# Attention and two MoE layers on one core: the second token block worked in two halves, the value sums taken by a selector product, and a new order of the work

## The chip, the cores and the metric

The kernel runs on one core of one Trainium2 chip, and the metric is the device time of one execution in microseconds (us). The engines are TensorE (PE, with its weight loads PEld), VectorE (DVE), ScalarE (ACT), GpSimd (POOL) and SyncE (SP), whose queue issues every DMA of this kernel. Each engine takes its own instructions in the order in which they are recorded, and waits on semaphores for the others.

## The reference

Eight heads of 64, two batches of 768 positions. A query sees the 31 positions nearest to it and, for every block of 32 positions, one summary: the block's maximal key (with log 32 added to the score) and the block's mean value. Two MLPs follow on all 1536 tokens of 512 columns.

```python
def _attn_ref(q, k, v):
    k_sum = k.reshape(B, H, nb, block, D).max(axis=3)
    v_sum = v.reshape(B, H, nb, block, D).mean(axis=3)
    scores_l = where(|i - j| < 16, q @ k.T / 8, -1e9)
    scores_s = q @ k_sum.T / 8 + log(32)
    a = softmax([scores_l, scores_s])          # sum + 1e-9
    return a @ [v, v_sum]
def _moe_ref(x, w_in, w_out):                  # 512 -> 2048 -> 512
    h = maximum(x @ w_in, 0); return (h * h) @ w_out
def _moe2_ref(x, w_in, w_out, g_ln):           # 512 -> 1024 -> 512
    h = x @ w_in; s = h * softmax(h)
    return ((s - mean(s)) / sqrt(var(s) + 1e-6) * g_ln) @ w_out
```

## The kernel before

**Blocks and units.** The 1536 tokens are three blocks of 512. Block 0 lies in batch 0, block 1 is the last 256 tokens of batch 0 and the first 256 of batch 1, block 2 lies in batch 1. Attention goes by units: a block and one of four pairs of heads. A unit needs its queries, the keys of its batch (loaded once per batch and pair, `load_k`), windows of values (`load_v`, into one of three buffers `vw`), and 24 rows of value sums, which `place_vs` copies under the values by DMA.

**Value sums.** `load_vst` brings 96 partitions (24 blocks by 4 heads) of 1024 numbers, half the positions of each block, into a buffer `kl` that it shares with the keys (two buffers in turn). `prep_vs` reduces them on DVE (L260), adds the second half (L262) and scales (L263). A unit holds two heads, one from each group of four, so its sums need all four loads of the batch.

**A unit's chain.** Scores of both heads on PE into two PSUM tiles (S), masking and row minimum on DVE (R, L310), exponentials on ACT (E, L318), reciprocal of the sum and scaling (n, N), transposes on PE (T) and their copy (C), products with the values (V), and the split of the result into a rounded part on ACT (H) and a residue on DVE (X). All MoE products use three terms: rounded by rounded, rounded by residue, residue by rounded.

**Weights.** They are stored as 64-bit words; each tile of 128x512 passes through ACT (a, L401), four DVE operations (b, c, d, e: L404, L408, L415, L418), a rounding (F) and a residue (f).

**First MoE.** `passes` names (block, phase) pairs; phases hold 6, 6 and 4 of the 16 column groups of the hidden layer. A step is 12 products `mm1` (M, L468), relu (U), square and residue (G, D), and 12 products `mm2` (O, L497) of 512 columns into four accumulators; 48 steps in all.

**Second MoE.** Twelve tiles of 128 tokens. `ysplit` (z) rounds a tile on ACT and takes its residue on POOL; `mm3` is 24 products (L543); `solu` (u) is a chain on DVE and ACT with one power on POOL (L566); `ln_tr` is eight transposes (L580); `mm4` is 24 products (L603). From tile 1 on the loop in `moe2` writes the order; tile 0 (i0, i1) stands in the table.

**What sets the order.** The table `ORDER`, written out by hand or planner, is recorded token by token: a letter (above), a number, and for some the engine (`d` DVE, `a` ACT, `p` POOL). `lk`, `lq`, `lv`, `ls`, `l` are loads, `y` a value sum, `P` `place_vs`, `k`, `K`, `m`, `q`, `Q`, `w` the preparation of keys and queries. `B4` is four products of the identity with itself (`warm`, L298) that nobody reads. SP issues the loads in the same order, with waits for the buffer to be free.

Of the kernel before, what the change touches and what calls it, by code (L numbers as in the profile page):

```python
# [21 lines left out]
ls0 lk0 lq0 lg0 l0 y0d lv0 B4 k0 lk1 k1 K0d K1d lq1 B1 q0 m0 ls1 Q0d w0a B7 S0 R0 l1 a0 R1 E0 b0 c0 d0 lv1 E1 e0 n0  # L22
N0d F0a n1 B14 k2 N1d k3 T0 K2d f0p lk2 T1 K3d C0a q1 m1 C1a lq2 Q1a y1d w1p l2 a1 b1 B8 S1 ls2 c1 d1 lv2 e1 F1d R2
f1p B5 k4 R3 E2 k5 K4d lk3 B1 q2 K5d E3 m2 lq3 n2 l3 N2d a2 n3 w2a B6 T2 y2d N3p C2a Q2a b2 ls3 c2 B6 S2 d2 e2 R4 F2a
B1 k6 k7 K6a f2d lk4 K7a R5 B1 q3 E4 lq4 Q3d m3 a3 E5 n4 w3p l4 y3d N4p B13 k8 k9 P0 K8a n5 N5d K9a ls4 B1 q4 lk5 m4
Q4a b3 l5 a4 w4p B4 V0 P1 T3 y4d H0 lv3 T4 C3a C4a B1 S3 lq5 X0 c3 k10 R6 K10a ls5 a5 R7 B2 V1 P2 E6 d3 T5 e3 k11 C5a
n6 l6 N6d E7 lk6 b4 B3 T6 b5 lq6 c4 q5 d4 C6a F3a n7 N7d H1 B2 V2 e4 K11a P3 Q5a c5 S4 lv4 f3p m5 H2 a6 y5d T7 F4a w5p
C7a l7 R8 ls6 f4p lq7 B7 V3 R9 E8 d5 k12 k13 e5 K12a q6 lk7 K13a n8 X1 F5a N8p H3 X2 lv5 E9 f5p X3 B4 T8 m6 M0 a7 n9
w6p y6d C8a l8 Q6a lq8 S5 U0a N9d G0 ls7 k14 b7 M1 b6 K14a c6 D0p R10 lv6 R11 E10 c7 k15 d6 T9 E11 e6 q7 O0 F6d l9 d7
C9a n10 Q7a N10d lq9 U1a n11 e7 G1 M2 N11d f6d a8 D1p y7d F7a K15a f7p T10 l10 a9 S6 C10a m7 P4 U2a q8 G2 R12 w7p M3  # L30
lq10 R13 E12 D2p E13 V4 P5 U3d n12 T11 a10 w8p O1 lv7 H4 C11a X4 Q8a b9 N12p P6 V5 n13 G3 N13d b8 T12 c8 H5 T13 c9
C12a O2 d8 C13a e8 X5 F8a lv8 D3d f8d S7 P7 d9 e9 q9 w9a R14 O3 lq11 R15 l11 E14 F9d f9d P8 b10 V6 Q9a c10 E15 d10 M4
e10 lv9 n14 H6 n15 F10a N14p X6 a11 l12 N15d T14 f10p U4d S8 C14d G4 b11 M5 R16 w10p P9 R17 E16 D4d l13 q10 a12 c11
# [26 lines left out]
def attn_moe_kernel(ctx, tc, q, k, v, w_in, w_out, w2_in, w2_out, g_ln, out):  # L60
# [13 lines left out]
    GB = 4  # L74
    NFC = DFF // P
# [42 lines left out]
    ap = actx.enter_context(tc.tile_pool(name="ap", bufs=1, side="right"))  # L118
    rctx = ExitStack()
# [4 lines left out]
    def consts():  # L124
        make_identity(nc, ident)
        nc.gpsimd.memset(mhalf, -0.5)
        nc.gpsimd.memset(one, 1.0)

        nc.gpsimd.memset(strip[:, :, 0:WK], 0.0)
        nc.gpsimd.memset(strip[:, :, WK:WN], 8.0 * LOGB)  # L130
        for h in range(2):
            r = strip[64 * h:64 * h + 64, :, 0:WK]

            nc.gpsimd.affine_select(out=r, in_=r, compare_op=ALU.is_gt, fill=-8.0 * BIG, base=0,
                                    pattern=[[0, 3], [1, WK]], channel_multiplier=-1)
# [18 lines left out]
    units = [(t, hp) for t in range(NT) for hp in range(HP)]  # L154

    segs = []
    for t in range(NT):
        segs.append([])
        lo = t * TB
        while lo < (t + 1) * TB:  # L160
            hi = min((t + 1) * TB, (lo // S + 1) * S)
            segs[t].append((lo // S, lo % S, (lo - t * TB) // 64, (hi - lo) // 64))
            lo = hi

# [39 lines left out]
    def prep_q0(u):  # L204
# [40 lines left out]
    def prep_vs(i, pool=False):
        b, h, half = i // 4, i // 2 % 2, i % 2
        n = HP * NSUM
        x = vst_t.pop(i)[0:n]
        if i % 4 == 0:
            vs[b] = ap.tile([n, 2, D], F32, name="vs", bufs=2)  # L250
        s = vs[b][:, h]
        o = s if half == 0 else ap.tile([n, D], F32, name="vs1", bufs=2)
        if pool:
            w = 512
            while w >= D:
                r = o if w == D else x[:, 0:w]
                nc.gpsimd.tensor_tensor(out=r, in0=x[:, 0:w], in1=x[:, w:2 * w], op=ALU.add)
                w //= 2
# [42 lines left out]
    EDGE = {(0, 0): 1, (1, 0): 1, (1, GB - 1): 2, (2, GB - 1): 2}  # L301

    def att_r(g):
        t, hp = units[g // 2]
        ps = ps_t.pop(g)
# [408 lines left out]
```

## Time and profile before

| | us |
|---|---|
| three runs | 514.0, 514.32, 516.18 (median 514.32) |
| the profiled execution, device time | 514.84 |
| its span in the trace | 512.7 |
| PE busy | 485.4 (95%), 2990 products |
| DVE busy | 349.5 (68%) |
| ACT busy | 236.0 (46%) |
| POOL busy | 127.0 (25%) |

The first product of the first MoE (M0) starts at 68.57 us, and attention and MoE products are mixed until about 158 us. From 161 us to the end of the first MoE at 372 us, and from 390 us to 509.6 us, PE has hardly a gap. A share over the whole span therefore hides that the first 70 us are another stage: there PE is busy with fillers (`warm` is 182 of the records, 26.9 us), while DVE is busy 97% of the time from 20 to 40 us.

### The profile page before, as it was taken

What the parts mean: (1) busy time and instruction counts of PE and PEld (TensorE: products, weight loads), DVE (VectorE), ACT (ScalarE), POOL (GpSimd) and SP (SyncE); (2) the same over time, 40 slices, a digit from 0 to 9 for tenths busy, and PEclk for the clock granted to TensorE, in tenths of its full rate; (3) what the DMA queues carried; (4) which work ended last, traced back from release to release, by engine and by line L of the source; (5) the groups of instructions that cost most, each with busy time, mean ns of one, the idle gap of its engine ahead of it and who ended that gap; (6) DMA issues with size and microseconds to landing.
All of it is one profiled execution on the core that took longest, in us unless ns stands there. A gap on an engine that the chain in (4) does not pass through costs nothing.

```text
span 512.7 us, 8027 instructions
## 1 busy us (share of the span) xinstructions
PE 485.4 (95%) x2990; PEld 405.5 (79%) x2990; DVE 349.5 (68%) x748; ACT 236.0 (46%) x526; POOL 127.0 (25%) x137
## 2 busy tenths in 40 slices
PE   6787787999999999999999999999999999999997
PEld 5786666787878888888888888888777888888886
DVE  4996997698971569962017979979187877665560
ACT  2464786679682545243235544575422242222231
POOL 2223443331210225112224244332312211210000
PEclk9897999999999999999999999999999999999999
DMA  8988889474720043360000514322000001000011
GB/s 176 239 208 187 187 196 223 89 175 140 189 57 0 2 123 83 105 179 4 0 1 0 166 42 124 122 91 75 0 2 0 22 21 42 20 22 20 22 41 41
DMA packets 59590, 44.03 MB, mean 86 GB/s; under 512 B 46624, under 2 KB 49184, under 8 KB 59552
## 3 DMA queue, kind: packets, MB, share of 16 engines
q1 hardware_dynamic: 59552, 43.53, 33.9%
q8 instruction: 23, 0.38, 0.3%
q14 instruction: 15, 0.12, 0.1%
HBM read 39.19 MB, written 3.15 MB: 83 GB/s over the span
## 4 chain that ended last, share of the span: by engine, by line
PE 68%; DVE 8%; DMA 8%; issue 5%; SPq 5%; ACT 4%; POOL 1%; ACTq 0%; POOLq 0%
PE acc L497 21%; PE h L468 21%; PE po L603 13%; PE h L543 8%; DMA st<-in_moe_w_in_dram 4%; PE lt L580 2%; DMA vw<-vs 2%; SPq L201 2%; DVE vs L260 1%; DMA kl<-in_v_dram 1%; PE at L349 1%; DMA kl<-in_k_dram 1%; SPq L174 1%; ACT sm L318 1%; ACT wf L401 1%
## 5 line engine op out<-in xcount | busy, mean ns | idle before, releaser
L468 PE MATMUL h<-xh,wi 128*128 128x512 f32 x384 | 128.5, 396 | 1.6 <-ACT r L475 1.6
L497 PE MATMUL acc<-gh,wo 128*128 128x512 f32 x384 | 126.6, 391 | 0.0
L468 PEld LDWEIGHTS h<-xh,wi 128*128 128x128 f32 x384 | 72.8, 190 | 17.3 <-ACT r L475 1.8
L497 PEld LDWEIGHTS acc<-gh,wo 128*128 128x128 f32 x384 | 72.1, 188 | 15.1 <-issue 0.2
L468 PE MATMUL h<-xl,wi 128*128 128x512 f32 x192 | 75.2, 392 | 0.0
L497 PE MATMUL acc<-gl,wo 128*128 128x512 f32 x192 | 74.8, 389 | 0.0
L89 POOL TENSOR_TENSOR gl<-r,gh 128x512 fp32r<-128x512 f32 x29 | 39.5, 1361 | 138.7 <-ACT r L484 96.0
L543 PE MATMUL h<-w,wf 128*128 128x512 f32 x288 | 67.8, 390 | 1.4 <-POOL wf L89 0.6
L543 PEld LDWEIGHTS h<-w,wf 128*128 128x128 f32 x288 | 53.8, 188 | 13.5 <-POOL wf L89 1.1
L483 ACT ACTIVATE gh<-r 128x512 fp32r<-128x512 f32 x48 | 30.3, 631 | 54.8 <-DVE r L477 44.5
L401 ACT ACTIVATE wf<-st 128x512 f32<-128x512 f32 x48 | 31.9, 669 | 29.5 <-DMA st<-in_moe_w_in_dram 19.5
L477 DVE TENSOR_SCALAR r<-h 128x512 f32<-128x512 f32 x22 | 15.1, 687 | 41.7 <-PE h L468 41.7
L468 PEld LDWEIGHTS h<-xl,wi 128*128 128x128 f32 x192 | 36.5, 190 | 7.2
L497 PEld LDWEIGHTS acc<-gl,wo 128*128 128x128 f32 x192 | 36.1, 188 | 7.2
L418 DVE SCALAR_TENSOR_TENSOR wf<-st,wf 128x512 uint32<-128x512 uint32 x48 | 40.5, 850 | 1.1
L318 ACT ACTIVATE sm<-sm,mn 128x120 f32<-128x120 f32 x96 | 36.5, 386 | 7.9 <-DVE mn L310 7.9
L553 ACT ACTIVATE st<-h,nm 128x1024 f32<-128x1024 f32 x12 | 13.4, 1117 | 56.8 <-DVE nm L550 56.8
L415 DVE SCALAR_TENSOR_TENSOR wf<-st,wf 128x512 uint32<-128x512 uint32 x48 | 34.1, 713 | 0.9
L566 POOL TENSOR_TENSOR vr<-vr,mhalf 128x1 f32<-128x1 f32 x12 | 6.6, 550 | 111.2 <-DVE vr L565 111.2
L475 ACT ACTIVATE r<-h 128x512 f32<-128x512 f32 x26 | 15.5, 597 | 35.5 <-PE h L468 35.5
L484 ACT ACTIVATE r<-r 128x512 f32<-128x512 f32 x48 | 30.4, 633 | 1.5
L603 PE MATMUL po<-wo,lh 128*128 128x512 f32 (+1 forms) x104 | 30.1, 373 | 0.0
(112 smaller groups left out, 787.4 us busy)
## 6 DMA issues: line engine op xcount, KB each, us to landing
st<-in_moe_w_out_dram SPq DMA_DIRECT2D x24, 512.0 KB, 4.2
st<-in_moe_w_in_dram SPq DMA_DIRECT2D x32, 256.0 KB, 4.0
st<-in_moe_w_in_dram SPq DMA_DIRECT2D x8, 512.0 KB, 3.7
kl<-in_v_dram SPq DMA_DIRECT2D x8, 384.0 KB, 5.0
kl<-in_k_dram SPq DMA_DIRECT2D x16, 192.0 KB, 4.5
out_dram<-ob SPq DMA_DIRECT2D x11, 256.0 KB, 2.0
vw<-in_v_dram SPq DMA_DIRECT2D x16, 168.0 KB, 2.9
qr<-in_q_dram SPq DMA_DIRECT2D x16, 128.0 KB, 5.4
```

The source lines that it names most:

```text
L89: eng.tensor_tensor(out=lo, in0=x, in1=hi.bitcast(F32), op=ALU.subtract)
L318: nc.scalar.activation(out=sm[:, j], in_=sm[:, j], func=AF.Exp, bias=mn[:, j:j + 1], scale=-1.0, accum_out=su[:, j:j + 1])
L401: nc.scalar.activation(out=wf_t[n], in_=st_t[n].rearrange("p (n t) -> p n t", t=2)[:, :, 1], func=AF.Abs)
L415: nc.vector.scalar_tensor_tensor(out=w, in0=st[:, :, 0], scalar=29, in1=w, op0=ALU.logical_shift_right, op1=ALU.bitwise_or)
L418: nc.vector.scalar_tensor_tensor(out=w, in0=st[:, :, 1], scalar=0xC0000000, in1=w, op0=ALU.bitwise_and, op1=ALU.bitwise_or)
L468: nc.tensor.matmul(ps, wi[:, wsel, d, :], x[t][:, d, :], start=(n == 0), stop=(n == 3 * HP - 1))
L475: nc.scalar.activation(out=r_t[s], in_=h_t.pop(s), func=AF.Relu)
L483: nc.scalar.activation(out=gh, in_=r, func=AF.Square)
L484: nc.scalar.activation(out=r, in_=r, func=AF.Square)
L497: nc.tensor.matmul(acc_t[e], wo[:, wsel, e, :], x, start=(edge(s, -1) and i == 0), stop=(edge(s, 1) and i == 2))
L543: nc.tensor.matmul(h2[:, fs], x[:, c, :], w_t[NW1 + nh * NDC + c][:, wsel, :], start=(n == 0), stop=(n == 3 * NDC - 1))
L603: nc.tensor.matmul(po[:, ds], x[:, cs], w_t[NW1 + 8 + c][:, wsel, ds], start=(n == 0), stop=(n == 3 * NF2 - 1))
```

## The change

- `TOK` gives attention four blocks: 512, 256, 256 and 512 tokens. The two of 256 are the old block 1, cut at the border of the batches; their units have one group of four score blocks (both heads) instead of two. There are 16 units and, as before, 24 groups. `passes` runs the first phase of block 1 in two halves of 256 columns (6 steps each), so the steps are 54; later phases of block 1 are whole.
- The value sums: one load per batch and pair of heads, 96 partitions of 2 x 512 numbers; three halving additions on DVE or POOL (`sum_v0`); a product of a 96x24 selector with entries 1/32 (`sum_v1`); a copy of 24x128 numbers (`sum_v2`). A unit's sums need its own load alone. Of the eight chains of additions three are on DVE and five on POOL.
- The transposes of the first block's probabilities go to an accumulator tile instead of one of the three tiles `at`.
- `ysplit` is cut in two tokens, so that the residue of a tile (`Z`) has a place of its own in the table.
- `ORDER` is new from the first token to the second MoE; fillers go from 91 products to 24.

```diff
-ls0 lk0 lq0 lg0 l0 y0d lv0 B4 k0 lk1 k1 K0d K1d lq1 B1 q0 m0 ls1 Q0d w0a B7 S0 R0 l1 a0 R1 E0 b0 c0 d0 lv1 E1 e0 n0
+ls0 lk0 l0 lq0 y0d B3 j0 lk1 J0d k0 k1 K0d K1a m0 a0 b0 c0 B5 q0 l1 d0 e0 lq1 w0a Q0a B2 S0 lk2 k2 k3 R0 E0 K2d ls1
...
-f45p O45 U46d b47 G46 f46p c47 M47 D46d d47 e47 g47 z0 i0 F47a U47a f47p G47 O46 D47d z1 i1 O47 z2 u0 Ya47 Yd47
+g46 i1 G53 D53d a47 b47 f45p F46d f46d z1 z2 c47 d47 e47 Z2p u0 O53 Yd53 g47 Z1p F47a f47p Ya53
...
+    TOK = (0, TB, S, 2 * TB, 3 * TB)
...
+        nc.gpsimd.memset(sel, 1.0 / 32.0)
...
+        nc.sync.dma_start(out=x[0:HP * NSUM].rearrange("p (h x) -> p h x", h=2),
+                          in_=ap_of(v[b, hp], 0, [[8 * D, HP * NSUM], [HP * S * D, 2], [1, 8 * D]]))
+
+    def sum_v0(i, eng):
+        x = vst_t[i][0:HP * NSUM].rearrange("p (h r d) -> p h r d", h=2, d=D)
+        for r in (4, 2, 1):
+            eng.tensor_tensor(out=x[:, :, 0:r], in0=x[:, :, 0:r], in1=x[:, :, r:2 * r], op=ALU.add)
+
+    def sum_v1(i):
+        b, hp = i // HP, i % HP
+        x = vst_t.pop(i)[0:HP * NSUM].rearrange("p (h r d) -> p h r d", h=2, d=D)
+        ps = acc_tile() if i < HP else ps_at.tile([P, 512], F32, name="at")
+        kq_t["v", i] = ps
+        nc.tensor.matmul(ps[32 * hp:32 * hp + NSUM, 0:P], sel, x[:, :, 0], start=True, stop=True)
+
+    def sum_v2(i, eng):
...
+        eng(vs[b][r], kq_t.pop(("v", i))[r, 0:P])
...
-        else:
-            nc.vector.tensor_reduce(out=o, in_=x.rearrange("p (j d) -> p d j", d=D), op=ALU.add, axis=AX.X)
-        if half == 1:
-            nc.vector.tensor_tensor(out=s, in0=s, in1=o, op=ALU.add)
-            nc.vector.tensor_scalar(out=s, in0=s, scalar1=1.0 / 32.0, scalar2=None, op0=ALU.mult)
...
-        ps = ps_at.tile([P, 512], F32, name="at")
+        ps = acc_tile() if units[groups[g][0]][0] == 0 else ps_at.tile([P, 512], F32, name="at")
...
-    passes = [(0, 0), (1, 0), (2, 0), (2, 1), (1, 1), (0, 1), (0, 2), (1, 2), (2, 2)]
-    steps = [(pi, sum(PHASE[:ph]) + i) for pi, (t, ph) in enumerate(passes) for i in range(PHASE[ph])]
+    HALF = ((1, 0, TB // 2), (1, TB // 2, TB))
+    FULL = tuple((t, 0, TB) for t in range(NT))
+    passes = [(x, 0) for x in FULL[:1] + HALF + FULL[2:]] + [(FULL[t], ph) for ph, t in ((1, 2), (1, 1), (1, 0), (2, 0), (2, 1), (2, 2))]
+    steps = [(x, sum(PHASE[:ph]) + i) for x, ph in passes for i in range(PHASE[ph])]
...
-                nc.tensor.matmul(ps, wi[:, wsel, d, :], x[t][:, d, :], start=(n == 0), stop=(n == 3 * HP - 1))
+                nc.tensor.matmul(ps[:, 0:hi - lo], wi[:, wsel, d, :], x[t][:, d, lo:hi], start=(n == 0), stop=(n == 3 * HP - 1))
...
-        split_lo(nc.gpsimd, yl, src, yh)
+        yhl[i] = (yh, yl, src)
+
+    def ysplit_lo(i, eng):
+        yh, yl, src = yhl[i]
+        split_lo(eng, yl, src, yh)
         yhl[i] = (yh, yl)
```

Three places show how the order moves. The first is DVE at the start, from the first value sum to the first masking of scores (ISA), as it was; kl is the loaded values, kT and ks keys and their block maxima, qT queries, wf a weight tile.

```order
L260 TENSOR_REDUCE vs<-kl 96x64
L631 COPY kT_93<-acc_167 128x384
L631 COPY kT_93<-acc_174 128x384
L191 TENSOR_REDUCE ks_98<-kT_93 128x24
L631 COPY qT_103<-acc_184 128x512
L310 ISA sm,mn<-at,strip 128x120
```

And as it is after the change:

```order
L242 TENSOR_TENSOR kl<-kl 96x2x256
L242 TENSOR_TENSOR kl<-kl 96x2x128
L242 TENSOR_TENSOR kl<-kl 96x2x64
L676 COPY vs<-acc_167 24x128
L676 COPY kT_94<-acc_174 128x384
L207 TENSOR_REDUCE ks_99<-kT_94 128x24
L440 TENSOR_SCALAR wf<-wf 128x512
L444 TENSOR_SCALAR wf<-wf 128x512
L451 SCALAR_TENSOR_TENSOR wf<-st,wf 128x512
L454 SCALAR_TENSOR_TENSOR wf<-st,wf 128x512
L337 ISA sm,mn<-at,strip 128x120
```

The reduction is three additions, one copy of keys and the copy of queries have gone to ACT, and the first weight tile stands ahead of the scores instead of behind them.

The second is POOL where the second MoE begins, before. A wf on the left with y on the right is the residue of a tile of 128 tokens (tiles 0, 1, 2, 3 in the order of the rows, y being the first block's output); vr is the power in the chain of `solu` of tile 0, then of tile 1; wo is the residue of a weight tile.

```order
L89 TENSOR_TENSOR wf_3676<-y_1774,wf_3675 128x512
L89 TENSOR_TENSOR wo_3695<-wf_3632,wo_3695 128x512
L89 TENSOR_TENSOR wf_3718<-y_1774,wf_3717 128x512
L89 TENSOR_TENSOR wf_3746<-y_1774,wf_3745 128x512
L566 TENSOR_TENSOR vr_3763<-vr_3763,mhalf_60 128x1
L89 TENSOR_TENSOR wf_3811<-y_1774,wf_3810 128x512
L566 TENSOR_TENSOR vr_3828<-vr_3828,mhalf_60 128x1
```

After the change, where tile 0 is wf_3818, tile 1 is wf_3916 and tile 2 is wf_3919:

```order
L94 TENSOR_TENSOR wf_3818<-y_1707,wf_3817 128x512
L94 TENSOR_TENSOR wo_3888<-wf_3769,wo_3888 128x512
L94 TENSOR_TENSOR wf_3919<-y_1707,wf_3918 128x512
L610 TENSOR_TENSOR vr_3939<-vr_3939,mhalf_60 128x1
L94 TENSOR_TENSOR wf_3916<-y_1707,wf_3915 128x512
L94 TENSOR_TENSOR wo_3961<-wf_3908,wo_3961 128x512
L94 TENSOR_TENSOR wf_4004<-y_1707,wf_4003 128x512
L610 TENSOR_TENSOR vr_4021<-vr_4021,mhalf_60 128x1
```

The residue of tile 1 has moved from two places ahead of the power of tile 0 to the place right behind it; that of tile 2 is ahead of it still.

The third is PE at the first products of tile 1 (the loop's first), after the change; PE's rows are the same in both kernels there, apart from numbers. acc are the last accumulations of the first MoE, h2 the hidden layer of the second, w2 its weights.

```order
L537 MATMUL acc3_3756<-gh_3903,wo_3372 128x512
L537 MATMUL acc3_3756<-gl_3904,wo_3372 128x512
L537 MATMUL acc3_3756<-gh_3903,wo_3372 128x512
L587 MATMUL h2_3978<-w2_3374,wf_3915 128x512 x2
L587 MATMUL h2_3978<-w2_3374,wf_3916 128x512
L587 MATMUL h2_3978<-w2_3376,wf_3915 128x512 x2
```

Nothing has moved here: the third product of tile 1 reads wf_3916, as the third product read that tile's residue (wf_3718) before.

## Rows read from the trace of the kernel before

**Rows 1.** Busy time, clock and DMA rate by stretch, from the windows view.

```profile
core 0: us, PE busy (x) PEld busy (x) DVE busy (x) ACT busy (x) POOL busy (x), PEclk, DMA share, GB/s
12.62:68.57 55.95, 43.18 (x511) 39.72 (x510) 50.91 (x155) 34.03 (x114) 18.07 (x20) 0.91 0.96 208
68.57:122.93 54.36, 49.73 (x485) 40.08 (x484) 43.10 (x139) 39.89 (x118) 20.94 (x22) 0.97 0.75 162
```

**Rows 2.** Groups by line, DVE, 0 to 68.57 us: busy us, mean ns.

```profile
L260 DVE TENSOR_REDUCE vs<-kl 96x64 f32<-96x1024 f32 x6 | 11.4, 1907 | 5.9 <-DMA kl<-in_v_dram 5.9
L191 DVE TENSOR_REDUCE ks<-kT 128x24 f32<-128x768 f32 x6 | 5.7, 947 | 0.1
L328 DVE TENSOR_TENSOR sm<-sm,su 128x480 f32<-128x480 f32 x6 | 5.3, 885 | 0.2
L418 DVE SCALAR_TENSOR_TENSOR wf<-st,wf 128x512 uint32<-128x512 uint32 x6 | 4.8, 795 | 0.2
L415 DVE SCALAR_TENSOR_TENSOR wf<-st,wf 128x512 uint32<-128x512 uint32 x6 | 4.1, 690 | 0.1
L631 DVE COPY kT<-acc 128x384 f32<-128x384 f32 x6 | 3.1, 553 | 0.9 <-PE acc L183 0.8
L408 DVE TENSOR_SCALAR wf<-wf 128x512 uint32<-128x512 uint32 x6 | 2.7, 446 | 0.1
L404 DVE TENSOR_SCALAR wf<-wf 128x512 f32<-128x512 f32 x6 | 2.4, 416 | 0.0
L631 DVE COPY qT<-acc 128x512 f32<-128x512 f32 x2 | 1.4, 685 | 0.0
L262 DVE TENSOR_TENSOR vs<-vs,vs 96x64 f32<-96x64 f32 x3 | 0.7, 222 | 0.1
```

**Rows 3.** Waits of DVE, 12.62 to 68.57 us: total, times, longest.

```profile
DVE sm L310 <- PE at L289: 3.7, 2, 2.1
DVE vs L260 <- DMA kl<-in_v_dram: 2.2, 1, 2.2
```

**Rows 4.** DVE and POOL in order of time near 17 us: start, us.

```profile
16.50 0.16 DVE L323 TENSOR_SCALAR su<-su 128x4 f32<-128x4 f32 x1
17.48 1.23 DVE L323 TENSOR_SCALAR su<-su 128x4 f32<-128x4 f32 x1
17.33 1.36 POOL L89 TENSOR_TENSOR wi<-wf,wi 128x512 fp32r<-128x512 f32 x1 [12.77 <-ACT wi L634]
```

**Rows 5.** Groups by line, POOL, 0 to 68.57 us.

```profile
L328 POOL TENSOR_TENSOR sm<-sm,su 128x480 f32<-128x480 f32 x3 | 3.0, 998 | 7.7 <-DVE su L324 4.1 <-PE at L334 3.6
```

**Rows 6.** The chain that ended last, late pieces: start, us.

```profile
485.72 5.46 PE po L603 x24
498.38 11.22 PE po L603 x72
```

**Rows 7.** PE, DVE and POOL in order of time, second MoE's beginning.

```profile
361.36 2.58 PE L543 MATMUL h<-w,wf 128*128 128x512 f32 x10 [0.62 <-POOL wf L89]
371.93 11.05 PE L543 MATMUL h<-w,wf 128*128 128x512 f32 x48
384.33 5.69 PE L543 MATMUL h<-w,wf 128*128 128x512 f32 x24 [0.48 <-DVE st L554]
390.42 1.09 PE L580 MATMUL lt<-ident,st 128*128 128x128 f32 x8 [0.39 <-DVE ll L89]
369.41 1.22 DVE L550 TENSOR_REDUCE nm<-h 128x1 f32<-128x1024 f32 x1 [6.30 <-PE h L543]
375.49 0.56 POOL L566 TENSOR_TENSOR vr<-vr,mhalf 128x1 f32<-128x1 f32 x1 [9.99 <-DVE vr L565]
376.01 1.30 POOL L89 TENSOR_TENSOR wf<-y,wf 128x512 fp32r<-128x512 f32 x1
```

**Rows 8.** Two windows of three microseconds, columns as in Rows 1.

```profile
45.00:48.00 3.00, 3.00 (x39) 2.88 (x36) 1.49 (x1) 0.85 (x2) 0.00 (x0) 0.50 1.16 250
48.00:51.00 3.00, 3.00 (x39) 2.47 (x38) 1.40 (x4) 0.94 (x2) 0.00 (x0) 0.52 1.17 193
```

More of the change, by code (lines that the diff above doesn't have):

```diff
@@ L152, in attn_moe_kernel, with size @@
     xh, xl = {}, {}
-    units = [(t, hp) for t in range(NT) for hp in range(HP)]
+    NTA = len(TOK) - 1
+    units = [(t, hp) for t in range(NTA) for hp in range(HP)]
     segs = []
-    for t in range(NT):
+    for t in range(NTA):
         segs.append([])
[L159 to L162, printed above, removed]
+        lo = TOK[t]
+        while lo < TOK[t + 1]:
+            hi = min(TOK[t + 1], (lo // S + 1) * S)
+            segs[t].append((lo // S, lo % S, (lo - TOK[t]) // 64, (hi - lo) // 64))
             lo = hi
+    def size(t):
+        return TOK[t + 1] - TOK[t]
     def kslot(b, hp):
@@ L241, in place_vs @@
         for b, s0, b0, nb in segs[t]:
-            src = vs[b].rearrange("p h d -> p (h d)")[NSUM * hp:NSUM * hp + NSUM]
+            src = vs[b][32 * hp:32 * hp + NSUM]
             nc.sync.dma_start(out=vw[u % NVB][WK:WN, b0:b0 + nb], in_=src.unsqueeze(1).to_broadcast([NSUM, nb, P]))
[L245 to L258, printed above, removed]
-        else:
-            nc.vector.tensor_reduce(out=o, in_=x.rearrange("p (j d) -> p d j", d=D), op=ALU.add, axis=AX.X)
-        if half == 1:
-            nc.vector.tensor_tensor(out=s, in0=s, in1=o, op=ALU.add)
-            nc.vector.tensor_scalar(out=s, in0=s, scalar1=1.0 / 32.0, scalar2=None, op0=ALU.mult)
     def prep_kw(u, eng):
@@ L277, in block @@
     def block(t, c, j):
-        return ((1 - c) if t == 1 else c) * GB + j
+        return c * (size(t) // P) + j
+    groups = []
+    first_g = []
+    for u, (t, hp) in enumerate(units):
+        first_g.append(len(groups))
+        if size(t) < TB:
+            groups.append((u, [(h, j) for h in range(2) for j in range(2)]))
+        else:
+            groups += [(u, [(h, j) for j in range(GB)]) for h in range(2)]
     def att_s(u):
         kw = kw_t.pop(u)
+        t = units[u][0]
         ps = [ps_at.tile([P, 512], F32, name="at") for _ in range(2)]
-        for j in range(GB):
+        for j in range(size(t) // P):
             for h in range(2):
@@ L344, in att_v @@
         ps = acc_tile() if t == 0 else ps_at.tile([P, 512], F32, name="at")
-        for j in range(GB):
+        where = {}
+        for g in range(first_g[u], len(groups)):
+            if groups[g][0] == u:
+                pt = pt_t.pop(g)
+                where.update({x: pt[:, i * P:(i + 1) * P] for i, x in enumerate(groups[g][1])})
+        for j in range(size(t) // P):
             for c in range(2):
@@ L480, in gsplit @@
         r = r_t.pop(s)
[L481 to L482 removed]
+        gh = gp.tile([P, TB], F32R, name="gh", bufs=2)[:, 0:width(s)]
+        gl = gp.tile([P, TB], F32R, name="gl", bufs=2)[:, 0:width(s)]
         nc.scalar.activation(out=gh, in_=r, func=AF.Square)
```

148 lines of the change are left out of this document (80 added, 68 removed).

## The prediction

> **What bounds the kernel now.** I read four views, from the coarse to the fine. First the shares by stretch, because 95% of the span on PE hides two different stages. From the first masking of scores at 12.62 us to the first product of the first MoE (M0) at 68.57 us, DVE is busy 50.91 of 55.95 us, PE 43.18 with its fillers, and the DMA queues 0.96 of the time [rows 1]. There the order of limits is DVE and the loads, and PE waits. In the next stretch PE is busy 49.73 of 54.36 us and DVE 43.10: PE binds, DVE is close behind it [rows 1]. Behind attention the chain of waits is PE without a gap; its long pieces are runs of products [rows 6]. So a microsecond of DVE counts in full until M0, a microsecond of PE counts in full from M0 on, and only waits of PE count at the end.
>
> Second, the groups of DVE before M0: the six reductions for the value sums are by far the dearest line, 11.4 us [rows 2]. Third, what DVE waits for there: 3.7 us for scores, 2.2 for a value load [rows 3]. Fourth, the beginning of the second MoE instruction by instruction: PE waits three times, 0.62 us for the residue of tile 0, then 0.48 and 0.39 [rows 7].
>
> All durations are of the one profiled execution: 514.84 us, 2.14 above its span and 0.5 above the median of the three runs. I take the sum against 514.84 and then 0.5 off.
>
> **Part 1: M0 comes earlier.** I count what DVE issues ahead of M0 in both orders and price it by [rows 2].
> - Removed: six reductions 11.4, the additions of the second halves 0.7, and the scalings, which no row here shows; they have the same 96x64 numbers, so I take 0.6. Together -12.7.
> - Added: four of the eight chains of additions stand ahead of M0, two on DVE and two on POOL. A chain adds 512, 256 and 128 numbers per partition. No row shows it. Below: three instructions at the 0.222 of 64 numbers, 0.7. Above: a line through 0.222 for 64 and 0.885 for 480 numbers gives 0.94 + 0.53 + 0.32 = 1.8. I take 1.4, nearer to the row of the same operation with the larger tile: +2.8 for two, with ends +1.3 and +3.6. One copy of sums, about 0.2.
> - Weights: fewer tiles are made ahead of M0: one b, c and d less and two e, 0.416 + 0.446 + 0.690 + 2 x 0.795 = -3.1.
> - Copies: keys on DVE go from six to ten, +2.2. Two copies of transposes move to DVE, at the 0.685 of 512 numbers +1.4. Two half-width copies of queries, by the line through 0.553 (384) and 0.685 (512) 0.4 each, +0.8.
> - One scaling of probabilities (0.885) and one reduction of keys (0.947) less: -1.8.
>
> That is -10.2. The weight tile's four operations (2.35 us) that now stand ahead of the first scores fill part of the wait for them, 2.1 of the 3.7 us [rows 3]: between 0 and -2.1, I take -0.9. Together **-11.1**, M0 at 57.5. The loads allow this: up to the placing of the third unit's sums SP issues 2.36 MB less than before, which at 208 GB/s [rows 1] is 11.3 us.
>
> **Part 2: halves.** Six steps of 24 products become twice as many of 256 columns. In the late chain 24 products of 512 columns take 5.46 us, 0.2275 each; 72 products of which 24 are of 512 and 48 of 256 columns take 11.22, so one of 256 takes (11.22 - 5.46) / 48 = 0.120 [rows 6]. Two halves cost 0.013 more than a whole, 144 times: **+1.9**, on the stage that PE binds.
>
> **Part 3: selector products.** Four of the eight fall behind M0; a product of 128 columns took 1.09 / 8 = 0.136 [rows 7]: **+0.5**. The copies behind them lie beside PE.
>
> **Part 4: waits between M0 and the end of attention.** PE lost 54.36 - 49.73 = 4.6 us there [rows 1]. Below: all of it goes, -4.6. Above: the work that is only put off past M0 on DVE (weights 3.1, scaling and keys 1.8) comes back as waits, +4.9. The order was laid out anew, and DVE remains about as loaded as PE; I take **-1.0**, near the old loss.
>
> **Part 5: the residue of tile 0** is now recorded well ahead of tile 0's products, so the wait of 0.62 us [rows 7] goes: **-0.6**.
>
> **Part 6: a new stall on PE.** In POOL's new order the residue of tile 1 stands behind the power of tile 0, and POOL takes its work in order. In the trace of before, the last product of tile 0 ended at 369.21, where DVE's `nm` could start after it (369.41); the power came at 375.49, after POOL had waited 9.99 us for DVE, and a residue behind it ran from 376.01 to 377.31 [rows 7]. So the chain sets the residue of tile 1 to about 8.1 us behind the end of tile 0. PE, meanwhile, has 12 products left, 2.72 us (the 48 products begin at 371.93), and then tile 1, whose third product reads that residue: it is due at 2.72 + 2 x 0.2275 = 3.2 us. PE has nothing else in its order that it could pull ahead: it stands still for 8.1 - 3.2 = 4.9, **+5.0** with the semaphore. Behind it ACT and DVE have caught up, so the later waits of 0.48 and 0.39 go: **-0.9**. Then the clock: after waits in the first stage PE was busy the whole of 45 to 51 us and was granted 0.50 and 0.52, the lower level [rows 8]. If the same follows this stall, six microseconds at half speed lose 3; if nothing, 0. I take the middle, **+1.6**.
>
> **Fillers.** There are 24 of them instead of 91. They matter only ahead of M0, where DVE binds, so I cost the change at nothing. DVE's work is the cover; what it costs without that is the second rival.
>
> **Sum.** -11.1 + 1.9 + 0.5 - 1.0 - 0.6 + 5.0 - 0.9 + 1.6 = -4.6. 514.84 - 4.6 = 510.2, less 0.5: **510 us**. The ends differ from the values taken by -1.5 and +0.8 (chains), -1.2 and +0.9 (first tile), -3.6 and +5.9 (part 4), -1.6 and +1.4 (clock); as independent errors (the root of the summed squares) that is -4.4 and +6.1, 505.5 to 516 at the outside, and 507 to 514 as the forecast's own range for 8 times in 10.
>
> **Rivals.**
>
> *POOL's additions hold DVE up.* At 17.48 us an operation of DVE on 128x4 numbers took 1.23 us, while POOL subtracted 128x512 numbers from 17.33 on; the same line took 0.16 a microsecond earlier [rows 4]. If DVE stands still for the whole of each addition on POOL, two chains ahead of M0 cost it what POOL needs for them: 128x480 numbers took 0.998 [rows 5], so about 1.0 + 0.7 + 0.5 = 2.2 a chain, 4.4 in all: 514.4, no change. Against it: the additions replace other work of POOL there, which was busy 18.07 us and disturbed DVE already. The Trainium skill ("SBUF — State Buffer", section "Who interferes with whom") states that a DVE instruction with two SBUF inputs and a GpSimd instruction shut each other out for the whole of an instruction; by that rule the additions on DVE would hold POOL up as well. [...]
>
> *The clock stays low without fillers.* The fillers were PE's work in its waits, and 24 of 91 remain. If PE is granted half its clock from the first scores to M0, 45 us instead of the 6 of [rows 8], then the wait of 1.6 us for scores (3.7 less 2.1, [rows 3]) that DVE had beside the slow stretch repeats about 7.5 times: +12, 522 us, slower. It decides from 6.9 us of such waits on, where it brings 516.9. Against it: DVE, not PE, is late in this stage, and mean clock there was 0.91 though PE had 12.8 us without work. The Trainium skill ("TensorE: Matmul & The Clock Gate", section "What's actually happening") calls the slow clock the default, which activity lifts; the rows agree that the clock falls, and none shows this stage without fillers.
>
> *More is won.* The order takes away DVE's other waits as well (3.7 + 2.2 less the 0.9 counted and one unavoidable microsecond, 4.0: M0 at 53.5), and the clock does not fall in the stall (1.6): 504 us. For it: additions wait for one load, not two. Against: DVE's time busy is 91% there, and the queues were full 0.96 of the time.
>
> **How the numbers follow.** The forecast 0.51, POOL's additions 0.20, low clock 0.12, more won 0.17. A measurement of this kernel can tell about 0.5% from no change, so faster means under 511.75 and slower over 516.9. Faster: of the forecast's share 0.78, since 1.75 us is well inside its own range above, 0.40, and 0.17: 0.57. Slower: most of the low clock, 0.10, and 0.01 of POOL's: 0.11. The rest, 0.32, is no change. Range: the forecast's own, widened to 502 for the end of "more is won" and to 516 for POOL's additions with a late M0; low clock is left out.
>
> **What would show it.** M0 near 57.5 us, with DVE busy over 90% ahead of it; at 68 it is the first rival, or the second if the granted clock there is near 0.5. Products of 256 columns at 0.12 us. One wait of PE near 5 us for POOL's residue at the beginning of the second MoE, no waits of 0.48 and 0.39 behind it, and a granted clock under 0.8 in the six microseconds after it. The forecast is wrong if that stall is missing (the time is then near 503.5) or if PE waits more than 6 us between M0 and the end of attention.

## The result, and the profile after

The changed kernel took 508.19 us in the median (506.61 to 508.38) against 514.16 for the kernel before on the same chip: ratio 0.9869, 95% interval 0.9837 to 0.9901, so 6 us faster, where 4.3 were forecast. In two later comparisons on other occasions the changed kernel had 505.96 (ratio 0.9814, 0.9767 to 0.9862) and 506.32 us (0.9823, 0.9768 to 0.9879). The profiled execution took 506.61 us with a span of 504.9; before, 514.84 and 512.7. The span is 7.8 us shorter, and these 7.8 us are taken apart here; the other three executions of that comparison had spans of 506.2 to 506.7, which is why the median moved by 6.0 only.

The first MoE begins earlier. The rows of its first product line (first and last start) and the stretches, columns as in [rows 1]:

```profile
L505 PE MATMUL h<-xh,wi x432: 277/389/504, 56.6 to 346.4; 128*128 128x512 f32 x112, 128*128 128x256 f32 x32
```

```profile
core 0: us, PE busy (x) PEld busy (x) DVE busy (x) ACT busy (x) POOL busy (x), PEclk, DMA share, GB/s
12.60:56.60 44.00, 30.60 (x412) 24.83 (x401) 40.61 (x148) 34.06 (x118) 15.79 (x16) 0.88 1.12 212
56.60:111.00 54.40, 53.66 (x488) 42.68 (x488) 48.40 (x149) 44.46 (x131) 22.16 (x21) 1.00 0.79 167
111.00:160.00 49.00, 49.00 (x537) 46.01 (x530) 32.60 (x106) 30.93 (x96) 12.40 (x14) 1.00 0.39 95
```

M0 starts at 56.6 us instead of 68.57. DVE is still busy 92% ahead of it: the stage has become shorter, its limit has not changed. Behind M0 PE loses 0.7 of 54.4 us, where it lost 4.6 before, and nothing from 111 to 160 us; its mean granted clock is 1.00 instead of 0.97 [rows 1].

The new additions among DVE's groups before M0 (busy, mean ns), and the copy of the sums, to be held against [rows 2]:

```profile
L242 DVE TENSOR_TENSOR kl<-kl 96x512 f32<-96x512 f32 x2 | 1.4, 686 | 3.6 <-DMA kl<-in_v_dram 3.6
L242 DVE TENSOR_TENSOR kl<-kl 96x256 f32<-96x256 f32 x2 | 0.8, 421 | 0.1
L242 DVE TENSOR_TENSOR kl<-kl 96x128 f32<-96x128 f32 x2 | 0.6, 289 | 0.1
L676 DVE COPY vs<-acc 24x128 f32<-24x128 f32 x1 | 0.3, 279 | 0.7 <-PE acc L249 0.7
```

A chain takes 0.686 + 0.421 + 0.289 = 1.40 us, against 1.91 for one reduction [rows 2].

The second MoE's beginning, in order of time (start, us, what ended the idle time before it); it answers to [rows 7]:

```profile
355.02 1.23 DVE L594 TENSOR_REDUCE nm<-h 128x1 f32<-128x1024 f32 x1 [0.99 <-PE h L587]
357.54 0.61 PE L587 MATMUL h<-w,wf 128*128 128x512 f32 x2
361.10 0.56 POOL L610 TENSOR_TENSOR vr<-vr,mhalf 128x1 f32<-128x1 f32 x1 [8.35 <-DVE vr L609]
361.62 1.27 POOL L94 TENSOR_TENSOR wf<-y,wf 128x512 fp32r<-128x512 f32 x1
362.95 13.58 PE L587 MATMUL h<-w,wf 128*128 128x512 f32 x46 [4.79 <-POOL wf L94]
377.16 5.70 PE L587 MATMUL h<-w,wf 128*128 128x512 f32 x24
```

PE starts tile 1 at 357.54, does two products, and stands still for 4.79 us until POOL has done the power and, behind it, the residue. Its next 46 products take 13.58 us; 48 of them (tiles 1 and 2) took 11.05 before. The windows across the stall tell why:

```profile
360.00:362.95 2.95, 0.00 (x1) 0.00 (x1) 2.10 (x8) 0.00 (x0) 1.85 (x3) 0.88 0.00 0
362.95:366.00 3.05, 3.05 (x7) 2.48 (x8) 3.05 (x4) 0.00 (x0) 2.80 (x2) 0.50 0.02 5
366.00:369.00 3.00, 3.00 (x8) 2.33 (x8) 1.07 (x2) 0.00 (x0) 0.00 (x0) 0.50 0.00 0
369.00:372.00 3.00, 3.00 (x14) 2.42 (x13) 0.88 (x1) 0.00 (x0) 0.00 (x0) 0.99 0.00 0
```

For the six microseconds after the wait PE is busy throughout and is granted half its clock: 15 products start in them, and 14 in the next three. That is the lower of its two levels, 1.2 of 2.4 GHz. The Trainium skill (page "TensorE: Matmul & The Clock Gate", section "What's actually happening") calls the slow clock the default, which activity lifts; these rows agree, with 0.50 behind the wait and 0.99 after six microseconds of work without a gap.

The sum by the two traces: M0 12.0 earlier; from M0 to the start of tile 1, 300.94 us (56.6 to 357.54) instead of 303.36 (68.57 to 371.93), 2.4 less; from there to the end 147.36 instead of 140.77, 6.6 more. -12.0 - 2.4 + 6.6 = -7.8.

### The profile page after: what moved, and what is told of

It is laid out like the page before. It is cut to its first block, busy times and chain, and to the rows that moved or that the text cites. A ratio compares the mean times of both kernels' runs of the same rounds, so it can differ in the third digit from the quotient of the medians.

```text
span 504.9 us, 8177 instructions
## 1 busy us (share of the span) xinstructions
PE 477.7 (95%) x3016; PEld 400.4 (79%) x3016; DVE 345.9 (69%) x766; ACT 246.7 (49%) x566; POOL 123.0 (24%) x134
## 4 chain that ended last, share of the span: by engine, by line
PE 80%; DVE 5%; DMA 5%; issue 3%; ACT 2%; SPq 2%; POOL 2%; POOLq 0%
PE h L505 24%; PE acc L537 23%; PE po L647 13%; PE h L587 12%; DMA kl<-in_v_dram 3%; PE lt L624 2%; PE at L381 2%; PE at L316 1%; PE at L361 1%; DMA kl<-in_k_dram 1%; POOL kl L242 1%; ACT sm L345 1%; PE at L225 1%; DVE wf L451 1%; DVE wf L440 1%
## 5 line engine op out<-in xcount | busy, mean ns | idle before, releaser
L505 PE MATMUL h<-xh,wi 128*128 128x512 f32 (+1 forms) x432 | 131.1, 369 | 0.0
L537 PE MATMUL acc<-gh,wo 128*128 128x512 f32 (+1 forms) x432 | 129.5, 367 | 0.0
L505 PE MATMUL h<-xl,wi 128*128 128x512 f32 (+1 forms) x216 | 79.0, 366 | 0.0
L537 PE MATMUL acc<-gl,wo 128*128 128x512 f32 (+1 forms) x216 | 79.0, 366 | 0.0
L94 POOL TENSOR_TENSOR gl<-r,gh 128x512 fp32r<-128x512 f32 (+1 forms) x27 | 34.1, 1264 | 139.4 <-ACT r L524 115.8
L523 ACT ACTIVATE gh<-r 128x512 fp32r<-128x512 f32 (+1 forms) x54 | 31.5, 583 | 35.4 <-DVE r L517 28.8
L515 ACT ACTIVATE r<-h 128x512 f32<-128x512 f32 (+1 forms) x32 | 18.0, 563 | 56.9 <-PE h L505 56.5
L451 DVE SCALAR_TENSOR_TENSOR wf<-st,wf 128x512 uint32<-128x512 uint32 x48 | 37.8, 789 | 1.1
L94 DVE TENSOR_TENSOR gl<-r,gh 128x512 fp32r<-128x512 f32 (+1 forms) x27 | 17.5, 648 | 27.9 <-ACT r L524 27.9
L524 ACT ACTIVATE r<-r 128x512 f32<-128x512 f32 (+1 forms) x54 | 31.7, 587 | 1.7
L627 ACT ACTIVATE lh<-lt 128x1024 fp32r<-128x1024 f32 x12 | 12.3, 1026 | 41.0 <-PE lt L624 41.0
```

What stands on the lines that cost most here:

```text
L94: eng.tensor_tensor(out=lo, in0=x, in1=hi.bitcast(F32), op=ALU.subtract)
L451: nc.vector.scalar_tensor_tensor(out=w, in0=st[:, :, 0], scalar=29, in1=w, op0=ALU.logical_shift_right, op1=ALU.bitwise_or)
L505: nc.tensor.matmul(ps[:, 0:hi - lo], wi[:, wsel, d, :], x[t][:, d, lo:hi], start=(n == 0), stop=(n == 3 * HP - 1))
L515: nc.scalar.activation(out=r_t[s], in_=h_t.pop(s), func=AF.Relu)
L523: nc.scalar.activation(out=gh, in_=r, func=AF.Square)
L524: nc.scalar.activation(out=r, in_=r, func=AF.Square)
```

## The experiments

Each ratio is to the kernel before, run on the same chip in the same comparison. The changed kernel was run again beside E5 to E7 (505.96 us) and beside E8 to E10 (506.32), but not beside E1 to E4; there it is compared by its ratios from the three other occasions, 0.9814 to 0.9869, whose intervals reach from 0.9767 to 0.9901.

**E1: the residue of tile 1 earlier.**

```diff
-g46 i1 G53 D53d a47 b47 f45p F46d f46d z1 z2 c47 d47 e47 Z2p u0 O53 Yd53 g47 Z1p F47a f47p Ya53
+g46 i1 G53 D53d a47 b47 f45p F46d f46d z1 Z1p z2 c47 d47 e47 Z2p u0 O53 Yd53 g47 F47a f47p Ya53
```

> The changed kernel with the residue of tile 1 recorded on POOL right behind its rounding, ahead of the power of tile 0, and nothing else. Theory (the stall and the clock behind it are the whole price of the second MoE's new order): PE's wait of 4.8 us is gone, the 48 products of tile 1 take 11.05 us again instead of 14.2, and waits of 0.5 and 0.4 come back behind them: 508.2 - 4.8 - 3.1 + 0.9 = 501.2 us. Rival (something else of that place is as late, such as the weights' residues or tile 2's, which now stand behind it): a wait over 2 us remains at the same place and the time is 504.5 or more.

(The 48 products are those of tiles 1 and 2.) Measured: 500.9 us, ratio to before 0.9711 (0.9696 to 0.9726). PE in order of time:

```profile
359.25 11.05 PE L587 MATMUL h<-w,wf 128*128 128x512 f32 x48
372.71 5.70 PE L587 MATMUL h<-w,wf 128*128 128x512 f32 x24 [1.54 <-DVE st L598]
378.80 1.09 PE L624 MATMUL lt<-ident,st 128*128 128x128 f32 x8 [0.38 <-DVE ll L94]
```

The wait and the slow stretch are gone, and 48 products take 11.05 us to the digit. The later waits come back, the first larger than before (1.54 against 0.48 [rows 7]): DVE's last output of the first MoE (2.47 us from 366.47 on) stands in front of tile 1's chain, which begins at 368.86. From tile 1 to the end the trace has 501.1 - 359.25 = 141.85 us, 5.5 less than the changed kernel. One token moved is worth nearly as much as the whole change brought, and this version beats both kernels, clear of their intervals.

**E2: the same stall in the kernel before.** `ysplit` is cut as in the change, for tile 1 alone.

```diff
-... F47a U47a f47p G47 O46 D47d z1 i1 O47 z2 u0 Ya47 Yd47
+... F47a U47a f47p G47 O46 D47d z1 i1 O47 z2 u0 Z1 Ya47 Yd47
...
```

> The kernel before with one edit: the residue of tile 1 is recorded on POOL behind the power of tile 0. Theory: the same price as in the changed kernel, 4.9 us of wait for the residue, 3.1 us of lower clock, 0.9 us of later waits gone: 514.2 + 7.1 = 521.3 us. Rival (the stall needs the rest of the new order, since in the order before other work lies between): not over 516 us.

Measured: 520.5 us against 516.05, ratio 1.0098 (1.0076 to 1.0119).

```profile
370.82 0.61 PE L551 MATMUL h<-w,wf 128*128 128x512 f32 x2
376.22 13.55 PE L551 MATMUL h<-w,wf 128*128 128x512 f32 x46 [4.79 <-POOL wf L89]
```

The same wait to the hundredth and the same slow stretch, without anything else of the change. From the start of tile 1 to the end the trace has 518.1 - 370.82 = 147.28 us, 6.5 more than before, where the changed kernel has 6.6 more. So the mechanism stands alone. The whole time grew by less than the 7.1 expected (4.5 by the medians, 5.1 by the ratio): the price behind tile 1 is 6.5, and this execution reached tile 1 1.1 us earlier (370.82 against 371.93).

**E3: the stall filled.** PE gets 16 products of the identity behind the last product of the first MoE, with a fresh PSUM tile to write to.

```diff
-... z1 z2 c47 d47 e47 Z2p u0 O53 Yd53 g47 Z1p F47a f47p Ya53
+... z1 z2 c47 d47 e47 Z2p u0 O53 Yd53 g47 Z1p F47a f47p Ya53 B16
...
+        if n == 16:
+            warm_t.clear()
```

> The changed kernel with 16 products of the identity with itself, which nobody reads, on PE between the last product of the first MoE and tile 1, where PE stands still for 4.8 us. Theory (the clock falls because PE stood still): the wait for the residue becomes shorter by what the products take (16 x 0.3 = 4.7 us), tile 1 starts at the same time as before this edit, its 48 products take about 11 us instead of 14.2: 508.2 - 3.1 = 505.1 us. Rival (the clock's fall there has another cause, or the products run at the lower clock themselves and last past the residue): 508 us or more.

Measured: 503.55 us, ratio to before 0.9767 (0.9747 to 0.9788); the changed kernel has 0.9814 to 0.9869. The changed kernel's intervals on two of the three occasions overlap this one, so the gain rests on the trace:

```profile
358.91 3.73 PE L327 MATMUL h<-ident 128*128 128x128 f32 x32
362.79 0.70 PE L589 MATMUL h<-w,wf 128*128 128x512 f32 x2
364.31 10.73 PE L589 MATMUL h<-w,wf 128*128 128x512 f32 x46 [0.82 <-POOL wf L94]
```

```profile
363.00:366.00 3.00, 2.18 (x9) 1.48 (x9) 2.91 (x3) 0.00 (x0) 2.92 (x4) 1.00 0.00 0
366.00:369.00 3.00, 3.00 (x15) 2.46 (x15) 2.45 (x5) 0.00 (x0) 1.21 (x1) 1.00 0.00 0
```

The residue comes no earlier, but 46 products take 10.73 us instead of 13.58 and the granted clock stays at 1.00. From where tile 1 could begin to the end it is 503.4 - 358.91 = 144.49 us, 2.9 less than the 147.36 of the changed kernel. So 2.9 us of the stall's price are clock, and they are due to PE having stood still. Fillers save these; only the earlier residue saves the wait as well.

**E4: no fillers at all.**

```diff
-ls0 lk0 l0 lq0 y0d B3 j0 lk1 J0d k0 k1 K0d K1a m0 a0 b0 c0 B5 q0 l1 d0 e0 lq1 w0a Q0a B2 S0 ...
+ls0 lk0 l0 lq0 y0d j0 lk1 J0d k0 k1 K0d K1a m0 a0 b0 c0 q0 l1 d0 e0 lq1 w0a Q0a S0 ...
...
```

> The changed kernel without any of its 24 products that nobody reads. Theory (DVE sets the time ahead of M0): M0 stays within 1 us of 56.6 us, 508.2 us within 1.5. Rival (the clock stays low without them and PE delays DVE): M0 later than 60 us, a mean granted clock below 0.8 from 13 to 56 us, 512 us or more.

Measured: 506.68 us, ratio 0.9821 (0.9796 to 0.9846), within the changed kernel's own. M0 stands at 58.7 us. The stretch ahead of it:

```profile
12.60:56.60 44.00, 33.69 (x380) 25.80 (x372) 39.50 (x145) 31.63 (x109) 13.48 (x15) 0.77 1.14 214
```

DVE's waits for scores ahead of M0 (total, times, longest), without fillers and, below it, in the changed kernel:

```profile
DVE sm L337 <- PE at L316: 3.1, 4, 1.7
DVE sm L337 <- PE at L316: 0.5, 1, 0.5
```

The mean clock is lower (0.77 against 0.88), DVE waits 3.1 us for scores instead of 0.5, and M0 is 2.1 us late, more than the theory's 1. So what the rival names does happen, but at a quarter of its 12 us, and no change of the time is shown. What half the clock through the whole stage would cost was not measured.

**E5 and E6: the additions all on DVE, all on POOL.**

```diff
-y2p ... y3p ... y4p ... y6p ... y7p
+y2d ... y3d ... y4d ... y6d ... y7d
```

> The changed kernel with all eight chains of additions on DVE instead of three. Two chains that stood on POOL ahead of M0 now cost DVE 2 x 1.46 us. Theory (DVE's own time sets M0, and POOL's additions held up DVE only now and then): M0 2 to 3 us later, the time 2 to 3 us longer than the changed kernel's. Rival (an addition on POOL stops DVE for its whole length, 2 x 2.7 us): M0 earlier by 2 us or more, and the time with it.

> The changed kernel with all eight chains of additions on POOL. Of the three taken off DVE the first stands where DVE waits for loads, the second ahead of M0 (1.46 us), the third behind M0. Theory (DVE's own time): M0 about 1 us earlier, the time 1 us shorter to unchanged. Rival (POOL's additions stop DVE): M0 1 to 3 us later, because a chain takes 2.7 us on POOL against 1.46 on DVE.

In E6 it is `y0`, `y1` and `y5` that go to POOL. Measured beside the changed kernel at 505.96 us: E5 508.29 (ratio to before 0.9857, 0.9809 to 0.9904), E6 507.47 (0.984, 0.9795 to 0.9885). M0 stands at 57.5 us in E5 and at 59.6 in E6; the three traces of the changed kernel have it at 53.6, 56.6 and 56.8. E5 is 2.3 us longer, as the theory has it, though the intervals overlap; E5's rival, an M0 earlier by 2 us, is out. E6 is 1.5 us longer instead of shorter, again inside the intervals, and its M0 is about as late as its rival says. Its trace shows another reason: the first chain ends later on POOL, and DVE waits for the product behind it:

```profile
DVE vs L676 <- PE acc L249: 7.2, 1, 7.2
```

That POOL's additions stop DVE for their whole length is so ruled out by E5. In the changed kernel's first trace DVE and POOL stand so in time:

```profile
29.24 2.61 POOL L242 TENSOR_TENSOR kl<-kl 96x512 f32<-96x512 f32 x3 [2.11 <-DMA kl<-in_v_dram]
34.49 0.66 DVE L355 TENSOR_TENSOR sm<-sm,su 128x480 f32<-128x480 f32 x1
37.57 0.69 DVE L451 SCALAR_TENSOR_TENSOR wf<-st,wf 128x512 uint32<-128x512 uint32 x1
37.61 3.11 POOL L242 TENSOR_TENSOR kl<-kl 96x512 f32<-96x512 f32 x3 [4.67 <-DMA kl<-in_v_dram]
42.22 1.27 POOL L94 TENSOR_TENSOR wi<-wf,wi 128x512 fp32r<-128x512 f32 x1 [1.49 <-ACT wi L679]
42.26 1.73 DVE L355 TENSOR_TENSOR sm<-sm,su 128x480 f32<-128x480 f32 x1
```

Beside the additions DVE keeps its durations here: L451 at 37.57 began 0.04 us ahead of them and took 0.69 us, and POOL's chain was the longer one, 3.11 us against 2.61 at 29.24. The scaling at 42.26 starts 0.04 us after POOL's residue and takes 1.73 instead of 0.66 us (the same line at 34.49). The trace of another execution of the same kernel, beside E8 to E10, has the additions in front:

```profile
36.71 3.10 POOL L242 TENSOR_TENSOR kl<-kl 96x512 f32<-96x512 f32 x3 [5.11 <-DMA kl<-in_v_dram]
37.05 1.65 DVE L451 SCALAR_TENSOR_TENSOR wf<-st,wf 128x512 uint32<-128x512 uint32 x1
```

There the same L451 begins 0.34 us after POOL's first addition and takes 1.65 us instead of 0.69; E1 and E3 have 1.65 and 1.77 at this place. So the additions do hold DVE up, but by one instruction, about 1 us, and only where one happens to begin behind an addition; the instruction that begins second is the one that takes longer.

**E7 and E8: the value sums alone, in the old order.** In the kernel before, each reduction becomes three additions on DVE, the selector product and the copy; E8 puts the last two later. In both, the first seven products write accumulator tiles, where the change does so for the first four.

```diff
 E7
-ls0 lk0 lq0 lg0 l0 y0d lv0 B4 k0 lk1 k1 ...
+ls0 lk0 lq0 lg0 l0 y0d j0 J0d lv0 B4 k0 lk1 k1 ...
...
 E8
-... C0a q1 m1 C1a lq2 Q1a y1d w1p l2 a1 b1 B8 S1 ...
+... C0a q1 m1 C1a lq2 Q1a y1d w1p l2 a1 b1 B8 j1 J1d S1 ...
...
```

> The kernel before in its own order, with the value sums of the change alone: each reduction replaced, at its place, by the three additions on DVE, the selector product on PE and the copy on DVE. Theory (the method saves DVE (1.91 - 1.46 - 0.28) x 6 + 1.3 = 2.3 us ahead of M0, the rest of the gain of 12 us comes from the order): M0 about 66 us, the time about 2 us shorter than before. Rival 1 (the method is most of the gain, since a unit needs its own load alone): M0 at 62 or earlier. Rival 2 (PE, which takes its work in order, now waits for the additions in front of scores): M0 not earlier.

> As e7, the kernel before with the value sums of the change alone, but each selector product stands later in PE's order, behind work that does not need it, and its copy with it. Theory (e7 lost its time because PE, in order, stood at the selector product until DVE had done the additions): PE's waits at that line fall from 21.4 us to under 5, M0 near 66 us, the time 0 to 3 us shorter than before. Rival (the method itself delays something else, such as the loads that share its buffers): 520 us or more although PE no longer waits there.

Measured: E7 530.47 us against 515.86, ratio 1.0299 (1.0242 to 1.0357); E8 522.66 against 514.71, 1.0141 (1.0094 to 1.0188). M0 stands at 81.3 and 73.3 us. PE's largest waits in E7:

```profile
PE acc L238 <- DVE kl L231: 21.4, 7, 6.5
```

In E8 PE, and SP's queue ahead of M0:

```profile
PE acc L247 <- DVE kl L240: 9.0, 4, 3.8
```

```profile
SPq L234 <- PE acc L247: 8.4, 3, 4.5
```

My theory for E7 was wrong and its second rival right: PE takes its work in order, and a selector product in front of scores holds them up until DVE, which is late, has done the additions. E8 shows that place decides (8 us won back), but it missed its theory, waits under 5 us and a time under the kernel before. The rival's 520 us came, but PE still waits 9.0 us, and the loads of values wait 8.4 us for buffers that the selector products now release. What the method saves with both removed stays open. Shown is that it saves nothing at the two places tried in the old order.

**E9: the transposes in the score tiles again.**

```diff
-        ps = acc_tile() if units[groups[g][0]][0] == 0 else ps_at.tile([P, 512], F32, name="at")
+        ps = ps_at.tile([P, 512], F32, name="at")
```

> The changed kernel with the transposes of the first block's probabilities in one of the three score tiles again, as before. Theory (the change of tile keeps scores from waiting for a free tile): PE waits 2 us or more for score tiles ahead of M0, M0 and the time 1 to 3 us later. Rival (three tiles suffice in the new order): the time within 1 us.

Measured: 507.48 us (0.9849, 0.9798 to 0.99) beside 506.32 for the changed kernel, M0 at 56.8 in both traces. The longest wait of PE there that can be one for a score tile is 1.2 us (PE at L361 <- DVE kT L676), not 2. The 1.2 us of time lie inside the intervals; no effect is shown.

**E10: no halves.** Block 1's first phase in six steps of 512 columns; the tokens of steps 6 to 11 leave, later ones are renumbered.

```diff
-    HALF = ((1, 0, TB // 2), (1, TB // 2, TB))
+    HALF = ((1, 0, TB),)
...
```

> The changed kernel with the second block's first phase in six steps of 512 columns, at the place of the second half, instead of twelve of 256; the rest of the order as it is. Theory (the halves give PE work while attention is still bound by DVE; that is why PE no longer waits between M0 and the end of attention): six half steps, 17 us of PE's work, are missing there, PE waits 5 to 10 us more, the halves' 1.9 us come back, and the time is 3 to 8 us longer. Rival (there is enough other work): 2 us shorter, by the price of the halves alone.

Measured: 517.63 us (1.0038, 1.0004 to 1.0073), 11.3 more than the changed kernel beside it, where the theory had 3 to 8. Its stretches, and PE's three largest waits from 56.6 to 160 us (total, times, longest):

```profile
56.60:111.00 54.40, 49.14 (x450) 37.46 (x449) 47.42 (x142) 43.64 (x129) 22.25 (x21) 1.00 0.73 169
111.00:160.00 49.00, 43.02 (x366) 34.39 (x365) 28.77 (x91) 23.35 (x74) 8.96 (x9) 0.93 0.40 82
```

```profile
PE at L306 <- DVE pt L666: 3.0, 1, 3.0
PE at L351 <- POOL sm L345: 1.8, 1, 1.8
PE at L351 <- ACT vs L669: 1.6, 1, 1.6
```

M0 is even earlier (54.5 us), yet PE stands still for 5.3 + 6.0 us between 56.6 and 160 us, where the changed kernel lost 0.7 and 0, and its mean clock is down to 0.93 in the second stretch. The waits are many and for all engines, and DVE is busy 87% of the first stretch but 59% of the second, so no single engine sets the pace there. That PE lacks products of the first MoE to do beside attention's chain is what the edit changed; that each wait comes of it is argued, not shown. In this order the halves are worth the whole gain; whether another order without them could give PE as much to do was not tried.

## Why the prediction was right, and where it was off

The time (508.2, forecast 510) and the shape were right. By the two traces M0 came 12.0 us earlier (part 1: 11.1), the stretch from M0 to tile 1 became 2.4 shorter (parts 2 to 5: 0.8 longer), and the rest 6.6 longer (part 6: 5.0 - 0.9 + 1.6 = 5.7). That the first and the last error, 0.9 each, cancel is luck; the middle one, 3.2 us, is the whole difference between -7.8 and -4.6. The median shows only 1.8 us of it, because the profiled execution of the changed kernel was the fastest of its four.

**M0.** Forecast 57.5, measured 56.6; the chain of additions 1.4, measured 1.40; the limit DVE, busy 92%. From 0 to M0, before and after:

```profile
0.00:68.57 68.57, 51.06 (x577) 46.99 (x577) 55.88 (x163) 36.98 (x118) 21.67 (x46) 0.93 0.94 202
0.00:56.60 56.60, 38.07 (x460) 31.42 (x460) 46.48 (x161) 38.10 (x124) 19.88 (x45) 0.91 1.09 207
```

DVE's work ahead of M0 fell by 9.4 us (forecast 10.2) and its idle time by 2.6 (forecast 0.9). The value sums make all of the 9.4: 12.7 us of DVE before (11.4 and 0.7 in [rows 2], and 0.6 for the scalings, of which the trace does have a row), 3.1 after (the rows of additions above); everything else together came to 0.2 more.

```profile
L263 DVE TENSOR_SCALAR vs<-vs 96x64 f32<-96x64 f32 x3 | 0.6, 201 | 0.1
```

How much the order and the four blocks of attention did to make this fit was not run apart: the new order with the old sums is missing.

But M0 turned out a poorer measure than I took it for, and that one trace lay within 1 us of the forecast is in part luck. The trace of a second execution of the same kernel had M0 at 53.6 and a span of 504.7, only 0.2 under the 504.9 of the one with 56.6; a third had 56.8 and 505.2; and E10 had it at 54.5 and was slower than the kernel before. What PE finds to do between M0 and the end of attention counts too (E10). And part 1 priced the new sums by DVE alone: that a selector product never holds PE up was taken for granted. In the changed order PE waits 7.7 us for additions ahead of M0, where it has the time; in the old order it waits 21.4 us for them, and the kernel is 14.6 us slower (E7). PE's waits of the changed kernel, 0 to 56.6 us:

```profile
PE acc L249 <- POOL kl L242: 4.2, 2, 2.3
PE acc L249 <- DVE kl L242: 3.5, 1, 3.5
```

**Halves and waits behind M0: the steps that were mis-sized.** The price of the halves was right. Eight products of 256 columns start from 97.62 to 98.58 us and so take 0.120 each:

```profile
97.62 0.40 PE L505 MATMUL h<-xh,wi 128*128 128x256 f32 x2
97.86 0.28 PE L505 MATMUL h<-xl,wi 128*128 128x256 f32 x1
97.98 0.40 PE L505 MATMUL h<-xh,wi 128*128 128x256 f32 x2
98.22 0.28 PE L505 MATMUL h<-xl,wi 128*128 128x256 f32 x1
98.34 0.40 PE L505 MATMUL h<-xh,wi 128*128 128x256 f32 x2
98.58 0.28 PE L505 MATMUL h<-xl,wi 128*128 128x256 f32 x1
```

But I booked them as a cost of 1.9 us and their use nowhere; part 4 gave -1.0 for all waits behind M0, from -4.6 to +4.9. PE's loss fell by 3.9 us, close to the lower end and 2.9 more than part 4 took, and that is most of the 3.2 us between -2.4 and +0.8. E10 points at the cause: without the halves PE loses 11.3 us between 56.6 and 160.

**The stall.** 4.9 forecast, 4.79 measured, in its place, for its reason, as E1, E2 and E3 show each from another side. The clock behind it costs 2.9 us, not 1.6: I took the middle between nothing and the six microseconds at half speed of [rows 8], and the upper end came. Fillers in PE's wait (E3) take it away, so standing still was the cause. The waits of 0.48 and 0.39 went, and so did that for tile 0's residue.

**The rivals.** *POOL's additions hold DVE up:* one instruction by about 1 us in some executions, not DVE for the length of the chains (E5 and the rows behind it). The line of [rows 4] on which this rival rests reads one tile (`su`) and is no case of two inputs; L355 and L451, which read two, were held up as well. *The clock stays low without fillers:* without the last 24 DVE waited 3.1 us for scores, under the 6.9 from which the rival decides (E4); the price of going from 91 to 24, which I put at nothing, was not run by itself. *More is won:* its M0 of 53.5 came in one trace of three, and the waits behind M0 went further than the forecast had them; but the clock did fall, which it put at nothing.

## What to carry to other kernels

When an engine takes its work in order, look at what stands in front of each short instruction that others wait for: a residue of 1.3 us behind a power that waits for a long chain cost 6.6 us, and moving its token won 5 to 8 us (ratio 0.9711 instead of 0.9814 to 0.9869). Price an edit that cuts work into pieces by what it lets begin earlier as well as by its overhead: the halves cost 1.9 us and were worth 11 in this order (E10). A new instruction on a waiting engine needs a place where its input is already there; the same sums were part of a faster kernel in one order and 14.6 us slower in another.

## What was not expected of the hardware

A wait of 4.8 us on a busy PE was followed by 6 us at half the granted clock, so it cost 2.9 us more than itself; in E3, with products nobody reads in most of the wait and 0.82 us of it left, the clock stayed at 1.00. And in these traces it is the one that begins second, of DVE and POOL, that takes longer: DVE's L451 took 0.69 us where it began 0.04 us ahead of POOL's additions, which then took 3.11 us against 2.61 for another such chain, and 1.65 us where it began 0.34 us behind them, in another execution of the same kernel. Which of the two came about was a matter of a third of a microsecond.
